# An unused tile of 192 bytes in front of the buffers of k, r and v

## The chip, the cores and the metric

The kernel runs on one core of one Trainium2 chip. The metric is the time of one execution on the device in microseconds (us); shorter is better. The core has five engines with an instruction stream of their own: TensorE (PE; its weight loads are listed as PEld), VectorE (DVE), ScalarE (ACT), GpSimd (POOL) and SyncE (SP), which here only issues DMAs. Tiles lie in the on-chip memory, in 128 partitions; matmul results go to eight PSUM banks, here one tile `banks`.

## The reference

Two layers, in float32, with a batch of B = 4 and S = 768 positions. First an attention with decay over H = 8 heads of D = 48, in which each position multiplies the state by w and adds k times v:

```python
for t in range(S):
    kt, vt, rt = (k[:, :, t], v[:, :, t], r[:, :, t])
    cur = np.einsum('bhd,bhe->bhde', u[None] * kt, vt)
    y[:, :, t] = np.einsum('bhd,bhde->bhe', rt, state + cur)
    state = w[None, :, :, None] * state + np.einsum('bhd,bhe->bhde', kt, vt)
```

Its output, with the heads side by side (384 columns), is the input x of a mixture of four attention experts with a head size of 64: a gate picks two of the four for each position, every expert computes causal softmax attention over the 768 positions, and the results are weighed and summed.

```python
for e in range(E):
    q, k, v = x @ wq[e], x @ wk[e], x @ wv[e]
    scores = np.where(causal, -1e9, scale * (q @ k.transpose(0, 2, 1)))
    a = softmax(scores)
    ye = a @ v @ wo[e]
    out += (weight of e among the two picked, else 0) * ye
```

## The kernel before

The positions are cut into 24 chunks of 128 (6 for each batch element), and these into 8 groups of three. A chunk n goes through the steps of the first layer, whose names begin with `a_`; a group G goes through those of the second, `m_`. A long string, `ORDER`, written out by hand, says in which order the steps issue their instructions, and so fixes the order on each engine. An engine works through its own list and waits on semaphores for what others make. The program gives its DMAs eight semaphores in turn, and an issue waits until the DMA eight before it has landed.

Loads. `load_chunk(n)` loads k (L287) and r (L289) of a chunk, and `load_vh(n)` v (L294), each as 128 partitions (positions) x 8 heads x 48 floats: 1024 rows of 192 bytes. All go through the queue of SyncE. k and r land in `kdbuf` and `rdbuf`, four buffers each, in which a head has 64 floats (256 bytes) of which 48 are filled; v lands in `vhbuf`, four buffers, in which the heads lie side by side (192 bytes each). `load_vs` (L308, L311) fills `vsbuf` with v, its two halves of 64 positions exchanged, for early chunks by a copy on ScalarE and later by DMAs. The weights come through the same queue: wv, wq, wk (`load_v`, `load_qk`) and wo.

The tiles are placed one behind the other in the order in which they are allocated. Ahead of `kdbuf0` this comes to an address of 128 modulo 256 bytes in each partition, and all buffers of k, r and v are multiples of 256 bytes long, so that each starts at 128 modulo 256.

```python
kdbuf = [const.tile([P, H, 64], F32, name=f"kdbuf{i}") for i in range(NK)]
vhbuf = [const.tile([P, H, D], F32, name=f"vhbuf{i}") for i in range(NV4)]
...
nc.sync.dma_start(kt[:, :, :D], k[b, :, s, :].rearrange("h s d -> s h d"))
nc.sync.dma_start(vh, v[b, :, c * C:(c + 1) * C, :].rearrange("h s d -> s h d"))
```

Steps of the first layer that the prediction names: `a_decay` multiplies k and r by tables of powers of w (L483 on GpSimd, L481 on VectorE for the first chunks); `a_ku` (L489, L491 on GpSimd) multiplies k, u and r; `a_transpose` (L519, L512 and L528 for chunk 0) turns k and r on TensorE by means of the identity, and ScalarE copies the result into `kr` (L255, the line of a helper); `a_quarters` (L557, L565), `a_out` (L588, L592) are its matmuls; `a_xt` (L623) turns the result into x. `fill` (L368), `warm_up` (L321) and `keep` (L362) are matmuls without use for the result, which keep TensorE at work at the start. Of the second layer: `hi_qk` (L440) copies wq and wk on ScalarE into a high part `wqk_hi`, the rest becomes `wqk_lo`; `m_values` (L692) and `m_proj` (L664) are projections with three matmuls each, high and low parts of x (`xt_hi`, `xt_lo`) and of the weights; `m_scores` (L742), `m_turn` (L777, with the identity), `m_av` (L798) and `m_out` (L821 to L823) are the attention and its output.

Of the kernel before, what the change touches and what calls it, by code (L numbers as in the profile page):

```python
# [7 lines left out]
F32 = mybir.dt.float32  # L8
# [182 lines left out]
def decay_attention_then_mixture_of_attention(  # L191
# [16 lines left out]
    B, H, S, D = r.shape  # L208
    E, DM, HD = wq.shape
    P = 128  # L210
# [15 lines left out]
    const = ctx.enter_context(tc.tile_pool(name="const", bufs=1))  # L226
# [30 lines left out]
    def load_w():  # L257
# [3 lines left out]
        for side_, rows in enumerate((lo_d, hi_d)):  # L261
            nc.scalar.dma_start(pw[rows, 0, :, 63], w.rearrange("(p two) d -> d two p", two=2)[:, side_])

    kdbuf = [const.tile([P, H, 64], F32, name=f"kdbuf{i}") for i in range(NK)]
    rdbuf = [const.tile([P, H, 64], F32, name=f"rdbuf{i}") for i in range(NR)]

# [615 lines left out]
```

## Time and profile before

| | |
|---|---|
| three runs | 303.3, 304.38, 302.42 us; median 303.3 us |
| the profiled execution | 303.65 us |
| its span, first to last instruction | 301.9 us |
| mean granted clock of TensorE | 0.994 |
| busy: PE, PEld, DVE, ACT, POOL | 96%, 83%, 77%, 61%, 58% of the span |
| read and written in DRAM | 19.28 MB and 4.72 MB |

The profile describes one execution by the hardware profiler. Its times count from the start of the span; the 1.75 us between the span and the execution's time lie before the first and behind the last instruction. Matmuls are pipelined and their ends are modelled, so a busy TensorE is not TensorE at its peak. The share of the DMA engines is a sum of the times of packets, which overlap.

### The profile page before, as it was taken

The page shows a single profiled execution, that of the slowest core. Times are in us where ns is not written, and L with a number is a line of the kernel's source. Part 1 is how long each engine was busy: PE and PEld are TensorE (multiplying, and loading weights), DVE is VectorE, ACT ScalarE, POOL GpSimd, SP SyncE. Part 2 cuts the span into 40 slices and gives each one's busy share as a digit, 9 for nine tenths or more (in the row PEclk, how much of TensorE's full clock was granted, in tenths as well). Part 3 has the DMA queues.
Part 4 walks back from the last instruction along what each step waited for, and adds up shares of the span by engine and source line. Part 5 has one row for each costly group of instructions (what it writes and reads, how often), then busy time and mean ns, then how long its engine had stood idle before and what let it go on. Part 6 is the DMA issues. An engine that isn't in the chain of part 4 may idle for free.

```text
span 301.9 us, 13029 instructions
## 1 busy us (share of the span) xinstructions
PE 291.0 (96%) x5565; PEld 251.1 (83%) x5565; DVE 232.5 (77%) x685; ACT 184.9 (61%) x413; POOL 174.3 (58%) x227
## 2 busy tenths in 40 slices
PE   6997999999999999999999999999999999999985
PEld 3776988898987979898987988997987979987865
DVE  5876498898886987868887788778887498889650
ACT  1864767657686564636867376664695864565722
POOL 1874798967574859376491973674745704226510
PEclk9999899999999999999999999999999999999999
DMA  9987954435088037535361248307070000010202
GB/s 131 180 170 155 158 106 84 79 60 81 28 157 161 2 64 137 111 73 126 80 134 25 48 88 161 73 4 158 12 164 2 28 2 4 0 54 2 77 31 78
DMA packets 103309, 24.83 MB, mean 82 GB/s; under 512 B 99794, under 2 KB 103252, under 8 KB 103252
## 3 DMA queue, kind: packets, MB, share of 16 engines
q1 hardware_dynamic: 102688, 23.90, 42.0%
q8 instruction: 43, 0.70, 1.0%
q10 hardware_dynamic: 564, 0.10, 0.2%
q14 instruction: 14, 0.11, 0.1%
HBM read 19.28 MB, written 4.72 MB: 79 GB/s over the span
## 4 chain that ended last, share of the span: by engine, by line
PE 79%; POOL 7%; DVE 5%; issue 4%; DMA 3%; ACT 0%; ACTq 0%; DVEq 0%; POOLq 0%; SPq 0%
PE banks L664 15%; PE banks L798 13%; PE banks L742 10%; PE banks L692 8%; PE banks L777 7%; PE banks L557 4%; PE banks L519 3%; PE banks L588 3%; PE banks L821 3%; PE banks L592 3%; PE banks L823 3%; PE banks L822 3%; PE banks L565 2%; DMA rdbuf<-in_r_dram 2%; PE banks L623 2%
## 5 line engine op out<-in xcount | busy, mean ns | idle before, releaser
L765 POOL TENSOR_SCALAR pr<-pr,f,gate 128x128 f32<-128x128 f32 (+5 forms) x96 | 68.1, 725 | 62.8 <-DVE f L759 40.1
L752 ACT ACTIVATE pr<-pr,nm 128x384 f32<-128x384 f32 (+5 forms) x96 | 63.2, 662 | 10.2 <-DVE nm L747 9.8
L747 DVE CUSTOM_DVE_ANT_0 pr<-banks,after 128x128 f32<-128x128 f32 (+5 forms) x96 | 55.8, 621 | 13.8 <-PE banks L742 11.3
L255 ACT ACTIVATE pt<-banks 128x768 f32<-128x768 f32 (+2 forms) x40 | 36.0, 910 | 23.6 <-PE banks L777 20.1
L798 PE MATMUL banks<-pt,vv 128*64 128x384 f32 (+2 forms) x324 | 41.5, 393 | 0.9 <-DVE yl L807 0.7
L742 PE MATMUL banks<-tk,tq 64*128 64x384 f32 (+3 forms) x384 | 41.7, 338 | 0.0
L798 PEld LDWEIGHTS banks<-pt,vv 128*64 128x64 f32 x324 | 22.7, 136 | 18.4 <-issue 11.8
L664 PE MATMUL banks<-xt_hi,wqk_hi 128*128 128x384 f32 x96 | 33.7, 351 | 0.0
L664 PE MATMUL banks<-xt_lo,wqk_hi 128*128 128x384 f32 x96 | 32.5, 338 | 0.0
L742 PEld LDWEIGHTS banks<-tk,tq 64*128 64x128 f32 x384 | 31.0, 187 | 1.8 <-issue 0.5
L664 PE MATMUL banks<-xt_hi,wqk_lo 128*128 128x384 f32 x96 | 32.4, 338 | 0.0
L489 POOL TENSOR_TENSOR ku<-kdbuf,uw 128x384 f32<-128x384 f32 x24 | 25.9, 1079 | 9.3 <-DVE banks L498 8.9
L483 POOL TENSOR_TENSOR rdbuf<-rdbuf,tab_r 128x384 f32<-128x384 f32 x22 | 22.5, 1023 | 14.1 <-DMA rdbuf<-in_r_dram 13.7
L777 PEld LDWEIGHTS banks<-ident,pr 64*128 64x128 f32 x672 | 25.4, 139 | 5.1 <-issue 1.8
L777 PE MATMUL banks<-ident,pr 64*128 64x64 f32 x672 | 29.0, 226 | 0.6 <-POOL pr L765 0.2
L588 PE MATMUL banks<-vhbuf,sm 64*64 64x48 f32 x384 | 24.6, 220 | 0.7 <-issue 0.6
L491 POOL TENSOR_TENSOR ku<-ku,rdbuf 128x384 f32<-128x384 f32 x24 | 24.3, 1012 | 1.2
L483 POOL TENSOR_TENSOR kdbuf<-kdbuf,tab_k 128x384 f32<-128x384 f32 x21 | 21.4, 1024 | 5.3 <-DMA kdbuf<-in_k_dram 4.0
L588 PE MATMUL banks<-vsbuf,sm 64*64 64x48 f32 x384 | 24.1, 220 | 0.0
L255 ACT ACTIVATE kr<-banks 128x1024 f32<-128x1024 f32 x19 | 19.4, 1022 | 7.0 <-PE banks L519 6.2
L692 PE MATMUL banks<-wv_hi,xt_hi 128*128 128x260 f32 x72 | 21.9, 304 | 0.0
L588 PEld LDWEIGHTS banks<-vhbuf,sm 64*64 64x64 f32 x384 | 20.5, 134 | 1.1 <-issue 0.9
(132 smaller groups left out, 722.4 us busy)
## 6 DMA issues: line engine op xcount, KB each, us to landing
kdbuf<-in_k_dram SPq DMA_DIRECT2D x24, 192.0 KB, 3.8
rdbuf<-in_r_dram SPq DMA_DIRECT2D x24, 192.0 KB, 4.1
vhbuf<-in_v_dram SPq DMA_DIRECT2D x24, 192.0 KB, 4.1
out_dram<-o SPq DMA_DIRECT2D x23, 192.0 KB, 2.3
vsbuf<-in_v_dram SPq DMA_DIRECT2D x36, 96.0 KB, 3.7
pr<-in_moe_wv_dram SPq DMA_DIRECT2D x1, 384.0 KB, 6.0
pr<-in_moe_wq_dram SPq DMA_DIRECT2D x1, 384.0 KB, 5.7
pr<-in_moe_wk_dram SPq DMA_DIRECT2D x1, 384.0 KB, 6.1
```

The lines of the kernel that those rows point to most:

```text
L255: nc.scalar.activation(to, from_, AF.Copy)
L483: nc.gpsimd.tensor_tensor(t[:, :, :D], t[:, :, :D], (tab_k, tab_r)[which], op=OP.mult)
L489: nc.gpsimd.tensor_tensor(ku, kd[:, :, :D], uw, op=OP.mult)
L588: nc.tensor.matmul(o, st["sm", n][rows, par, p // 2, i], values, start=fresh, stop=True)
L664: nc.tensor.matmul(ps, a[:, t, m0:m0 + P], x[:, t, :], start=i == 0, stop=i == n - 1)
L692: nc.tensor.matmul(ps, x[:, t, cols], a[:, t, :], start=m == 0, stop=m == n - 1)
L742: nc.tensor.matmul(ps[par][:, n0:n1], tq[rows, part, q], tk[rows, key, n0:n1], start=i == 0, stop=i == 2)
L747: nc.vector.tensor_tensor_reduce(pr_[:, :N], ps[par], after[:, S - N:], 1.0, 3e38, op0=OP.add, op1=OP.min, accum_out=nm)
L752: nc.scalar.activation(pr_[:, :N], pr_[:, :N], AF.Exp, bias=nm, scale=-1.0, accum_out=sums[:, e, j, 0:1])
L765: nc.gpsimd.tensor_scalar(p[:, :N], p[:, :N], f[:, i], gate[:, i, e:e + 1], op0=OP.mult, op1=OP.mult)
L777: nc.tensor.transpose(both[:, x, half], mg[G]["p", e, j][rows, i * C:(i + 1) * C], ident[rows, rows])
L798: nc.tensor.matmul(psy[par * HD:par * HD + HD, j0 * C:j1 * C], vv[:, i % GC, e, :], mg[G]["t", e, i][:, (j0 - max(0, i - g * GC)) * C:(j1 ...
```

## The change

One line allocates a tile of 48 floats (192 bytes) in each partition, which nothing uses. All tiles that are allocated after it move by 192 bytes: `kdbuf`, `rdbuf`, `vhbuf` and `vsbuf` from 128 to 64 modulo 256, and likewise, each from its own place, the identity, masks and tables, `uw`, the weights (`wqk_hi`, `wqk_lo`, `wv_hi`, `wv_lo`, `wo_hi`, `wo_lo`, `wg`) and `sums`. The tiles of the string of buffers `BUFS` (`pr`, `tq`, `kr`, `xt_hi` and so on) are allocated before it and stay. The instructions of each engine and their order are the same before and after, so no excerpt of them is shown.

```diff
             nc.scalar.dma_start(pw[rows, 0, :, 63], w.rearrange("(p two) d -> d two p", two=2)[:, side_])
 
+    const.tile([P, D], F32, name="space")
     kdbuf = [const.tile([P, H, 64], F32, name=f"kdbuf{i}") for i in range(NK)]
     rdbuf = [const.tile([P, H, 64], F32, name=f"rdbuf{i}") for i in range(NR)]
```

## Rows read from the trace of the kernel before

**Rows 1.** The page: busy time of TensorE, share of the span, instructions

```profile
PE 291.0 (96%) x5565; PEld 251.1 (83%) x5565; DVE 232.5 (77%) x685; ACT 184.9 (61%) x413; POOL 174.3 (58%) x227
```

**Rows 2.** The page: the chain that ended last, by engine and by line

```profile
PE 79%; POOL 7%; DVE 5%; issue 4%; DMA 3%; ACT 0%; ACTq 0%; DVEq 0%; POOLq 0%; SPq 0%
PE banks L664 15%; PE banks L798 13%; PE banks L742 10%; PE banks L692 8%; PE banks L777 7%; PE banks L557 4%; PE banks L519 3%; PE banks L588 3%; PE banks L821 3%; PE banks L592 3%; PE banks L823 3%; PE banks L822 3%; PE banks L565 2%; DMA rdbuf<-in_r_dram 2%; PE banks L623 2%
```

**Rows 3.** Windows: length; busy PE, PEld, DVE, ACT, POOL; granted clock; DMA share; GB/s

```profile
28.75:32.10 3.35, 3.35 (x49) 2.85 (x39) 1.35 (x3) 0.42 (x2) 2.45 (x3) 0.50 0.51 96
...
36.00:300.00 264.00, 260.78 (x4945) 227.17 (x4943) 208.00 (x627) 165.36 (x375) 151.62 (x191) 1.00 0.35 72
```

**Rows 4.** Timeline of TensorE, 24.5 to 33.3 us (start, length, instructions, [idle before <-releaser])

```profile
25.50 0.26 PE L588 MATMUL banks<-vhbuf,sm 64*64 64x48 f32 x2 [0.57 <-issue]
...
25.99 0.61 PE L368 MATMUL banks<-ident 128*128 128x256 bf16 x4
28.07 0.69 PE L557 MATMUL banks<-kr 48*64 48x64 f32 x32 [1.47 <-ACT kr L255]
28.58 0.77 PE L565 MATMUL banks<-vhbuf,kdbuf 64*48 64x48 f32 x32
...
29.88 0.42 PE L692 MATMUL banks<-wv_hi,xt_lo 128*128 128x260 f32 x1
...
33.16 0.28 PE L692 MATMUL banks<-wv_hi,xt_lo 128*128 128x260 f32 x1
```

**Rows 5.** Timeline of ScalarE, 19 to 29 us

```profile
23.54 0.84 ACT L440 ACTIVATE wqk_hi<-pr 128x768 fp32r<-128x768 f32 x1 [2.34 <-DMA pr<-in_moe_wq_dram]
...
26.26 0.84 ACT L440 ACTIVATE wqk_hi<-pr 128x768 fp32r<-128x768 f32 x1 [1.49 <-DMA pr<-in_moe_wk_dram]
27.01 1.01 ACT L255 ACTIVATE kr<-banks 128x1024 f32<-128x1024 f32 x1
```

**Rows 6.** Timeline of GpSimd, 19 to 40 us

```profile
25.17 0.51 POOL L615 TENSOR_TENSOR z<-z,w 128x192 f32<-128x192 f32 x1
29.65 1.02 POOL L483 TENSOR_TENSOR rdbuf<-rdbuf,tab_r 128x384 f32<-128x384 f32 x1 [3.98 <-DMA rdbuf<-in_r_dram]
...
38.31 1.03 POOL L483 TENSOR_TENSOR rdbuf<-rdbuf,tab_r 128x384 f32<-128x384 f32 x1 [2.35 <-DMA rdbuf<-in_r_dram]
```

**Rows 7.** DMA view, 0 to 13 us in 40 slices of 0.325 us

```profile
GB/s 0 0 0 0 0 9 67 182 253 204 240 137 140 161 175 178 220 209 179 161 164 167 162 161 166 162 163 163 166 161 163 165 175 207 218 212 204 219 181 160
```

**Rows 8.** DMA view, 29 to 36 us in 40 slices of 0.175 us

```profile
GB/s 11 26 26 9 0 0 0 0 46 92 117 192 257 261 236 214 206 170 174 202 204 190 184 171 163 159 134 149 190 187 167 164 160 257 154 150 157 151 161 165
```

**Rows 9.** DMA view, 40 to 53 us in 40 slices of 0.325 us

```profile
GB/s 0 0 67 219 240 114 69 92 225 194 96 120 235 226 244 226 176 162 184 158 79 0 0 0 0 0 0 0 0 25 0 50 34 103 235 233 249 204 91 27
```

**Rows 10.** Timeline of SyncE's queue, 29 to 47 us: issues

```profile
29.43 0.37 SPq L287 DMA_DIRECT2D kdbuf<-in_k_dram  x1
...
39.63 0.37 SPq L294 DMA_DIRECT2D vhbuf<-in_v_dram  x1
...
41.47 1.09 SPq L294 DMA_DIRECT2D vhbuf<-in_v_dram  x1
42.68 0.61 SPq L287 DMA_DIRECT2D kdbuf<-in_k_dram  x1
43.82 0.46 SPq L289 DMA_DIRECT2D rdbuf<-in_r_dram  x1
```

**Rows 11.** Timeline of TensorE, 89 to 92 us

```profile
90.93 0.46 PE L519 MATMUL banks<-ident,rdbuf 64*128 64x64 f32 x8 [0.50 <-POOL rdbuf L483]
```

**Rows 12.** The chain that ended last, in order of time (start, us, what)

```profile
1.71 3.96 DMA pr<-in_w_dram
...
84.45 5.33 DMA rdbuf<-in_r_dram
```

**Rows 13.** Weight loads of TensorE by form (xcount | busy us, mean ns | idle before)

```profile
L664 PEld LDWEIGHTS banks<-xt_lo,wqk_hi 128*128 128x128 f32 x96 | 18.1, 188 | 0.0
...
L822 PEld LDWEIGHTS banks<-wo_lo,yh 128*128 128x128 f32 x50 | 9.4, 188 | 0.0
```

## The prediction

> **What bounds the kernel now.** I read the page first. TensorE is busy for 291.0 of 301.9 us [rows 1], and the chain of work that ended last is 79% TensorE [rows 2]. So a change pays only where it closes a hole in TensorE's row or keeps TensorE's clock up. In the windows by stage, from 36 to 300 us TensorE is busy 260.78 of 264 us at a granted clock of 1.00 [rows 3]: 3.2 us are left in seven eighths of the run. The start is different. In the timeline of TensorE it stands idle for 1.47 us before 28.07, released by ScalarE's kr [rows 4]. From 28.75 to 32.10 the granted clock is 0.50, the lower of the two levels (1.2 against 2.4 GHz) [rows 3]; the fall comes right after that idle time. In it the L692 matmuls take 0.42 us each, at full clock 0.28 [rows 4].
>
> Why was kr late? In ScalarE's timeline the weights' split waits 2.34 us for the load of wq and 1.49 us for that of wk; kr stands right behind [rows 5]. GpSimd waits in the same stretch: 3.98 us for a load of r at 29.65, and 2.35 us for another at 38.31 [rows 6]. So the first 38 us wait for loads, and all loads go through one queue. The program gives its DMAs eight semaphores in turn, so an issue also waits until the DMA eight before it has landed: a load that lands sooner lets later ones start sooner.
>
> How fast does that queue run? In the DMA view of 0 to 13 us a slice is 0.325 us. By slice 19 (6.2 us) the slices sum to about 0.77 MB, nearly four loads of 196,608 bytes (k, r, v, k). Then come 13 slices at 161 to 167 GB/s, 0.69 MB, and behind them five at 204 to 219 [rows 7]; in the order of issue r, k and r stand there, and then two loads of v. The slices count what is read, and reads may run ahead of the writes for part of a load: a burst begins at 240 to 261 GB/s [rows 7, 8] and is then held back. So 163 GB/s is the pace at which rows of k and r are written, and some 212 that of v's. The other views agree. At 29 to 36 us five loads of k and r begin at 257 to 261 GB/s and sink to 134 to 204 [rows 8]. At 40 to 53 us loads of v (issued 39.63 to 41.47) and the front of a k are read at 226 to 244; behind k comes r (issued 42.68 and 43.82), at 158 to 184 [rows 9, 10]. k, r and v have the same shape in DRAM and the same 192-byte rows. What differs is where they land: rows of k and r lie 256 bytes apart from an address of 128 modulo 256, so each covers 128 to 320 and crosses a multiple of 256. Rows of v lie 192 bytes apart, start at 128, 64, 0 and 192 in turn, and half of them cross.
>
> **The change part by part.** *The unused tile.* No instruction writes or reads it, and no instruction is added, removed or reordered on any engine. Its cost is nothing.
>
> *Loads of k and r.* All 48 now land on 64 to 256 and none crosses. If a row costs by the blocks of 256 bytes that it touches, k and r cost 2, and v 1.5: 163 x 2 / 1.5 = 217 GB/s for v, where some 212 is the mean of its slices [rows 7]. One block would give 326 GB/s, which is more than the queue reads where nothing holds it back, 226 to 244 [rows 9]. So I take 212 to 240 GB/s for the new loads: 0.93 to 0.82 us in place of 1.21, and 0.28 to 0.39 us saved for each load in a full queue. That v's rate carries over to k and r is a reading, not shown: no row has k or r without a crossing.
>
> The Trainium skill ("DMA: Bandwidth & Descriptors", section "How a descriptor splits into AXI transactions") says that a descriptor is cut at multiples of 256 bytes, in beats of 32, and that a start off the boundary costs the beats before it too. Counted so, 128 to 320 takes 10 beats and 64 to 256 takes 8; at 163 x 10 / 8 = 204 GB/s a load would save 0.25 us, and the sum below would stand. The section speaks of reads; no row here shows whether it holds where a row is written.
>
> *Loads of v.* They start at 64, 0, 192 and 128: half cross, as before. Nothing.
>
> *The wait at 28.07.* Eight loads of k and r stand in the full queue ahead of the weights: 8 x 0.28 to 0.39 = 2.2 to 3.1 us sooner for wq, wk and what follows. For TensorE not to wait, kr must be done by 26.60, when it ends its fill (25.99 + 0.61) [rows 4]. kr takes 1.01 us and the split 0.84 [rows 5], so wk must be there by about 24.7, where it came at 26.2: 1.5 us sooner is enough. The whole 1.47 us go. ScalarE's own work leaves room (free at 21.2 us, 23.54 less the wait, and 2.0 us of work ahead of kr), so 0.7 to 1.6 us are to spare.
>
> *The clock.* With no hole before 28 us I take the fall as gone: 3.4 us at half clock (28.7 to 32.1) hold 1.7 us of full-clock work, so 1.7 us are saved. Bounds: 0 if it falls anyway, 1.7 if not. It is nearer to 1.7, because the one fall between 8 us and the end follows the one long hole.
>
> *Does the rest keep up?* GpSimd's r at 29.65 comes 2.2 to 3.9 us sooner (eight to ten loads); GpSimd is free at 25.7 [rows 6], so it gains at least 2.2. The r at 38.31 is the last of five k and r loads; the first of them is issued at 29.43 [rows 10], when TensorE's L565 of 28.58 [rows 4] has read the k of its buffer. That is 1.5 to 2 us sooner, and five loads give 1.4 to 2.0 more: 2.9 to 4.0. TensorE's 3.2 us can therefore be kept.
>
> *Later.* The hole of 0.50 us at 90.93 waits for GpSimd's rdbuf [rows 11], and that for a load of r that took 5.33 us [rows 12] with another r just ahead: two loads save 0.56 to 0.78, so the hole goes.
>
> *The front.* The chain begins with the small load of w, 3.96 us from issue [rows 12], queued among the first k and r: 0 to 0.5 us. I take 0, because ScalarE and a cold TensorE have work of their own there. The 0.57 us at 25.50 have no releaser [rows 4]: 0 to 0.57, taken as 0.
>
> *Operands.* Identity, masks, tables and weights move by 192 bytes too. A weight load from wqk (224 modulo 256) takes 188 ns and one from yh (128) 188 ns [rows 13]: nothing.
>
> Sum: 1.47 + 1.7 + 0.50 = 3.7 us off the profiled execution's 303.65 us: 299.95. Its own time stands 0.35 us above the median of the runs, 303.3, well inside their spread (302.42 to 304.38). I forecast **300.0 us**, 1.1% less. At best, with both terms taken as 0, it is 303.65 - 4.75 = 298.9.
>
> **The rivals.** *It speeds the loads less, or the clock falls anyway.* If a load saves 0.1 us, the hole shrinks by 0.8 and stays: 302.9. If the hole goes but the clock falls: 303.65 - 1.97 = 301.7. For it: the rows show the fall behind the hole, not that it comes from it alone. Range 301.3 to 302.9.
>
> *The change doesn't do what it says: the gap between rows, or their size, is what costs.* Rows of k and r leave 64 bytes free after each 192; v's rows do not. This explains 163 against 212 just as well. Then nothing moves and the time is 303.3. The Trainium skill (same page, "Specifications") has a rule on this side: transfers under 512 bytes are done as read-modify-write. 192 bytes stay under that at any address, and by that rule alone the time stays at 303.3; that v, with rows of the same size, runs at 212 speaks for the address having a part.
>
> *Slower: the operands that moved.* Transposes (L777, L519, L623) read the identity, now at 64 in place of 128. L777 and L519 alone hold 10% of the chain [rows 2], 31 us. If crossings are free and those take 10% longer, that is +3.1 us: 306.8. It outweighs the forecast's gain only beyond 12%. Rows 13 speak against it.
>
> **How the numbers follow.** A measurement of this kernel can tell about 1% (3 us) from no change. Forecast (298.9 to 301.3): 0.51. Smaller gain (301.3 to 302.9): 0.16. No change (302.4 to 304.4): 0.28. Slower (about 306.8): 0.05. The bound of 1% is 300.3, just above the forecast; of its 0.51 I put 0.37 below. The rest of it, the smaller gain and no change make 0.58 within 1%. The range runs from 298.8 (the forecast's best) to 303.9 (most of no change): it leaves out the slower case, the upper edge of no change and a little below, under 0.2.
>
> **What would show it.** In the DMA view of 0 to 13 us the slices at 161 to 167 become 204 or more; the loads of k show a shorter time to landing. ScalarE's waits for wq and wk shrink by 2 us or more together; the hole at 28.07 is gone, the granted clock stays at 1.00 past 28 us, and GpSimd's 3.98 us shrink below 2. Wrong would be: slices still at 163 (no change); faster loads with a hole as before (the queue was not what wk waited for); or a hole that opens at another place between 30 and 50 us, with the clock falling there.

## The result, and the profile after

| | before | after |
|---|---|---|
| median of 7 runs each, taken side by side | 303.92 us (302.42 to 304.69) | 300.32 us (298.62 to 301.77) |
| ratio after / before | | 0.9883, 95% interval 0.9844 to 0.9921 |
| the profiled execution, its span | 303.65, 301.9 us | 301.08, 299.3 us |
| busy TensorE, granted clock | 291.0 us, 0.994 | 287.7 us, 1.00 |

The change saves 1.2%, 3.6 us by the medians; the forecast was 300.0 us. The two profiled executions are 2.6 us apart, since the one of before is 0.3 us below its median and that of after 0.8 above, so what follows accounts for 2.6 us. The profile shows which of the terms behind the forecast held. Lines of code behind the new one stand one further down: L664 of before is L665 here.

The DMA view of 0 to 13 us, 40 slices of 0.325 us, answers to [rows 7]:

```profile
GB/s 0 0 0 0 0 11 92 185 247 178 238 213 179 233 242 193 201 199 206 234 197 171 174 193 219 240 151 142 203 202 189 214 193 244 206 182 193 190 203 211
```

The 13 slices at 161 to 167 are gone. Slices 20 to 32 (6.2 to 10.4 us) have a mean of 195 GB/s, where it was 163. The step on the pace held in direction, and fell short of the 212 to 240 that were taken.

ScalarE's timeline, 20 to 27 us, answers to [rows 5]:

```profile
22.14 0.85 ACT L441 ACTIVATE wqk_hi<-pr 128x768 fp32r<-128x768 f32 x1 [1.75 <-DMA pr<-in_moe_wq_dram]
...
24.77 0.84 ACT L441 ACTIVATE wqk_hi<-pr 128x768 fp32r<-128x768 f32 x1 [1.40 <-DMA pr<-in_moe_wk_dram]
25.52 1.00 ACT L255 ACTIVATE kr<-banks 128x1024 f32<-128x1024 f32 x1
```

wq comes 1.40 us sooner, wk 1.49 us; but what ScalarE has ahead of them came sooner too, so that the two waits shrank by 0.68 us together, not by 2. TensorE's timeline, 24 to 32 us, answers to [rows 4]:

```profile
24.13 0.26 PE L589 MATMUL banks<-vhbuf,sm 64*64 64x48 f32 x2 [0.34 <-issue]
...
26.57 0.69 PE L558 MATMUL banks<-kr 48*64 48x64 f32 x32 [1.34 <-ACT kr L255]
...
28.02 0.28 PE L693 MATMUL banks<-wv_hi,xt_hi 128*128 128x260 f32 x1
...
30.05 0.47 PE L520 MATMUL banks<-ident,kdbuf 64*128 64x64 f32 x8 [0.81 <-POOL kdbuf L484]
```

The hole before kr is still there: 1.34 us, where 1.47 stood before. And yet the clock doesn't fall behind it: L693 takes 0.28 us. A hole of 0.81 us that before did not have follows at 30.05. The windows say the same of the clock (length; busy PE, PEld, DVE, ACT, POOL; granted clock; DMA share; GB/s), beside [rows 3]:

```profile
28.75:32.10 3.35, 2.54 (x35) 2.25 (x34) 2.30 (x3) 2.09 (x4) 3.28 (x5) 1.00 1.02 204
36.00:295.00 259.00, 256.43 (x4923) 222.99 (x4922) 207.40 (x624) 162.51 (x367) 149.65 (x188) 1.00 0.33 71
```

GpSimd's timeline, 22 to 40 us, answers to [rows 6]: its two waits for r are 3.25 and 0.81 us, where they were 3.98 and 2.35.

```profile
28.01 1.02 POOL L484 TENSOR_TENSOR rdbuf<-rdbuf,tab_r 128x384 f32<-128x384 f32 x1 [3.25 <-DMA rdbuf<-in_r_dram]
...
34.61 1.02 POOL L484 TENSOR_TENSOR rdbuf<-rdbuf,tab_r 128x384 f32<-128x384 f32 x1 [0.81 <-DMA rdbuf<-in_r_dram]
```

The chain in order of time begins with the small load of w, as in [rows 12], now 3.14 us from issue in place of 3.96:

```profile
1.72 3.14 DMA pr<-in_w_dram
```

That load is issued by ScalarE while the first k and r are under way, and the chain goes on by VectorE and GpSimd to TensorE's L417 (L416 in the kernel before, at 9.90 us):

```profile
7.02 0.94 POOL L387 TENSOR_TENSOR w<-pr 128x2 f32<-128x2 f32 x3 [4.84 <-DVE pr L381]
...
9.08 0.91 PE L417 MATMUL banks<-pt,ones 1*128 1x384 f32 x2 [0.48 <-POOL lower L348]
```

Where is the time gained? TensorE's matmuls stand in the same order in both kernels (some small ones of L588 and L592, interleaved, apart), so the start of one and the same matmul can be compared. The table has the starts of five, in us from the start of the span:

| matmul | before | after | sooner |
|---|---|---|---|
| the 61st, first layer's values (11.25) | 11.25 | 10.43 | 0.82 |
| the 541st, behind the hole before kr | 28.64 | 27.14 | 1.50 |
| the 601st, in the first `m_values` | 33.16 | 31.05 | 2.11 |
| the 1201st | 57.68 | 54.66 | 3.02 |
| the last | 298.63 | 296.03 | 2.60 |

All of it is gained by 57 us: 0.8 us at the front; 0.7 up to kr, of which 0.13 is the hole before kr, 0.23 the idle time at 25.50 [rows 4] (0.57 us, now 0.34) and 0.29 comes between two matmuls of L588 at 20.67; 0.6 by the 601st; 0.9 between 33 and 57 us, 0.7 of that in three steps of 0.2 to 0.3 us at 48 to 52 us.

What sets the 0.6? In the kernel before, the transposes behind the stretch at half clock start at 32.17 us, with no idle time listed ahead of them. In this one they wait 0.81 us for GpSimd's kdbuf, and start 2.04 us after GpSimd takes up the r that it had waited for (28.01). A kernel of the experiments below, k and r at 192, has the pace of before and a clock of 1.00 throughout; there too it is 2.04 us (TensorE of before; GpSimd and TensorE of k and r at 192, where L519 is L521):

```profile
32.17 0.47 PE L519 MATMUL banks<-ident,kdbuf 64*128 64x64 f32 x8
```

```profile
29.86 1.01 POOL L485 TENSOR_TENSOR rdbuf<-rdbuf,tab_r 128x384 f32<-128x384 f32 x1 [4.11 <-DMA rdbuf<-in_r_dram]
```

```profile
31.90 0.46 PE L521 MATMUL banks<-ident,kdbuf 64*128 64x64 f32 x8 [1.22 <-POOL kdbuf L485]
```

So in the kernel before, where GpSimd takes up that r at 29.65 [rows 6], these transposes could have started at 31.69 at the earliest, whatever the clock: the fall held them up by 0.5 us. Of the 2.1 us gained here, 1.6 are those by which the r comes sooner.

Later the hole at 90.93 [rows 11] is gone, but two new ones, at 58.85 (no releaser) and at 119.97 (for VectorE's copy into an output buffer), take more than that away:

```profile
58.85 0.28 PE L693 MATMUL banks<-wv_lo,xt_hi 128*128 128x260 f32 x1 [0.58 <-issue]
...
119.97 1.05 PE L743 MATMUL banks<-tk,tq 64*128 64x384 f32 x6 [0.69 <-DVE o L253]
```

### The profile page after: what moved, and what is told of

The parts are those of the page before. It is cut to its first block, busy times and chain, and to the rows that moved or that the text cites. A ratio compares the mean times of both kernels' runs of the same rounds, so it can differ in the third digit from the quotient of the medians.

```text
span 299.3 us, 13029 instructions
## 1 busy us (share of the span) xinstructions
PE 287.7 (96%) x5565; PEld 248.3 (83%) x5565; DVE 233.3 (78%) x685; ACT 184.7 (62%) x413; POOL 173.1 (58%) x227
## 4 chain that ended last, share of the span: by engine, by line
PE 85%; POOL 5%; issue 3%; DMA 2%; DVE 2%; ACT 2%; ACTq 0%; POOLq 0%; DVEq 0%
PE banks L665 17%; PE banks L799 13%; PE banks L743 11%; PE banks L693 9%; PE banks L778 7%; PE banks L558 4%; PE banks L520 4%; PE banks L589 3%; PE banks L593 3%; PE banks L822 3%; PE banks L824 3%; PE banks L823 3%; PE banks L566 2%; PE banks L624 2%; POOL ku L490 2%
## 5 line engine op out<-in xcount | busy, mean ns | idle before, releaser
L665 PE MATMUL banks<-xt_hi,wqk_hi 128*128 128x384 f32 x96 | 33.5, 349 | 0.0
L665 PE MATMUL banks<-xt_hi,wqk_lo 128*128 128x384 f32 x96 | 32.3, 337 | 0.0
L665 PE MATMUL banks<-xt_lo,wqk_hi 128*128 128x384 f32 x96 | 32.3, 337 | 0.0
L490 POOL TENSOR_TENSOR ku<-kdbuf,uw 128x384 f32<-128x384 f32 x24 | 25.0, 1040 | 10.3 <-DVE banks L499 10.0
L589 PE MATMUL banks<-vhbuf,sm 64*64 64x48 f32 x384 | 24.4, 219 | 0.3 <-issue 0.3
L693 PE MATMUL banks<-wv_hi,xt_hi 128*128 128x260 f32 x72 | 21.5, 299 | 0.0
```

Source lines behind the costliest of these rows:

```text
L490: nc.gpsimd.tensor_tensor(ku, kd[:, :, :D], uw, op=OP.mult)
L589: nc.tensor.matmul(o, st["sm", n][rows, par, p // 2, i], values, start=fresh, stop=True)
L665: nc.tensor.matmul(ps, a[:, t, m0:m0 + P], x[:, t, :], start=i == 0, stop=i == n - 1)
L693: nc.tensor.matmul(ps, x[:, t, cols], a[:, t, :], start=m == 0, stop=m == n - 1)
```

## The experiments

### Which of the moved tiles, and which address

Four kernels came first. The first moves k and r alone and puts all else back:

```diff
+    const.tile([P, 48], F32, name="space")
     kdbuf = [const.tile([P, H, 64], F32, name=f"kdbuf{i}") for i in range(NK)]
     rdbuf = [const.tile([P, H, 64], F32, name=f"rdbuf{i}") for i in range(NR)]
+    const.tile([P, 16], F32, name="space_after")
```

> Only the buffers of k and r lie at 64 modulo 256; a second unused tile of 64 bytes behind them puts v, identity, masks, tables and weights back where they were. If crossings of k and r are the cause: as with the whole change, ratio 0.988 (0.984 to 0.992), slices of the DMA view of 0 to 13 us at 190 to 240 GB/s instead of 163, granted clock 1.0 or nearly. If the other tiles that moved have the gain: ratio 1.000, slices at 163 with k and r no matter.

The second leaves k and r at 128 and moves the rest (the 48 floats stand behind `rdbuf`):

> k and r stay at 128 modulo 256, all tiles behind them move by 192 bytes as in the change. If crossings of k and r are the cause: ratio 1.000 (0.996 to 1.004), slices at 161 to 167 GB/s, clock 0.994. If the other tiles have the gain: ratio 0.988.

The third and the fourth are the first with other numbers, so that k and r start at 0, or at 96, modulo 256, and all else stays where it was:

> k and r at 0 modulo 256, all else as before: rows cover 0 to 192, no crossing. By blocks of 256 bytes: as with the change, ratio 0.988, slices at 190 to 240. By beats of 32 bytes counted from the block's start (6 here, 8 at 64, 10 at 128): the same or a little better, since reads set the pace. If 64 were good for another reason than the crossing: 1.000 and 163.

> k and r at 96 modulo 256, all else as before: rows cover 96 to 288 and cross by 32 bytes. By blocks touched: as before the change, 161 to 167 GB/s and ratio 1.000. By beats counted from the block's start (9, against 10 at 128): 163 x 10 / 9 = 181 GB/s and about half the gain, 0.994.

| k and r at | the rest | median, us | ratio to before | mean of slices 20 to 32, GB/s |
|---|---|---|---|---|
| 64 | as before | 300.47 | 0.9889 (0.9802 to 0.9976) | 209 |
| 128 | moved | 303.8 | 0.9993 (0.9955 to 1.0031) | 163 |
| 0 | as before | 301.05 | 0.9876 (0.9811 to 0.9941) | 208 |
| 96 | as before | 304.52 | 1.0007 (0.9972 to 1.0043) | 163 |

The DMA view of 0 to 13 us of k and r at 64 and the rest as before, then of k and r at 128 and the rest moved:

```profile
GB/s 0 0 0 0 0 10 74 188 251 195 230 217 188 224 226 164 163 159 232 232 236 227 226 174 177 242 195 234 223 148 179 223 207 187 193 210 175 171 184 211
```

```profile
GB/s 0 0 0 0 0 12 88 174 248 201 213 167 151 183 166 186 218 201 173 161 165 165 162 164 165 162 163 163 165 162 163 165 186 209 217 217 192 202 167 226
```

Of k and r at 0:

```profile
GB/s 0 0 0 0 0 14 75 194 238 204 218 208 184 251 233 193 207 174 177 243 226 157 171 192 213 248 223 184 194 199 225 226 197 166 218 196 238 215 173 203
```

and at 96:

```profile
GB/s 0 0 0 0 0 12 88 193 240 208 232 149 140 165 164 188 216 207 177 160 162 167 161 164 164 161 164 164 164 164 162 166 178 212 219 216 217 215 183 180
```

The gain comes from k and r alone, and it comes at both addresses at which a row of 192 bytes stays inside one block of 256 bytes (64 to 256, 0 to 192). The moved identity, masks and weights neither cost nor give anything that can be told from no change (0.9955 to 1.0031). At 96 a row crosses by only 32 bytes and the pace is the same 163 GB/s as at 128, where it crosses by 64: what counts is that a second block is touched.

An experiment of the last set belongs here, k and r at 192, where the row is cut into 64 and 128 bytes (16 floats ahead of `kdbuf`, 48 behind `rdbuf`):

> The kernel before, with k's and r's buffers at 192 modulo 256, v and all else at 128: a row covers 192 to 384 and is cut into 64 and 128 bytes, where it was 128 and 64, and 160 and 32 with the buffers at 96. Theory A (a row costs by the blocks of 256 bytes that it touches, two in all three cases): slices at 161 to 167 GB/s from about 6.5 us on, no change of the time, ratio 0.996 to 1.004. Rival B (a row costs by 32-byte steps counted from the last multiple of 256 ahead of it, 12 here, 10 in the kernel before): 136 GB/s, and 2 us slower or more, 306 or above. Rival C (how the row is cut matters, the first piece above all): a pace other than 161 to 167 GB/s.

304.49 us, ratio 1.0003 (0.9973 to 1.0032), and a mean of 164 GB/s:

```profile
GB/s 0 0 0 0 0 14 65 190 250 215 225 141 144 169 166 188 214 202 175 153 170 171 165 164 164 162 164 163 164 163 164 164 181 208 218 212 191 209 173 179
```

So theory A: two blocks cost the same however the row is cut between them. The Trainium skill ("DMA: Bandwidth & Descriptors", section "How a descriptor splits into AXI transactions") has both counts: a descriptor is cut into transactions at multiples of 256 bytes, and each transaction costs beats of 32 bytes from the multiple below its start. By the beats the rows at 128, 96 and 192 would take 10, 9 and 12, and from 163 GB/s at 128 follow 181 and 136 (estimates by that page). The runs show 163 and 164: the cut into transactions agrees, the beats do not count here. The section speaks of reads; these rows are cut where they are written.

### k alone, r alone

```diff
+    const.tile([P, 48], F32, name="space")
     kdbuf = [const.tile([P, H, 64], F32, name=f"kdbuf{i}") for i in range(NK)]
+    const.tile([P, 16], F32, name="space_after")
     rdbuf = [const.tile([P, H, 64], F32, name=f"rdbuf{i}") for i in range(NR)]
```

> The kernel before, with k's buffers alone moved to 64 modulo 256 (the unused 192 bytes ahead of them, 64 more unused bytes ahead of r's buffers); r, v and all else stay at 128. So half the loads of the change are freed of crossings. Theory A (the gain is a sum over loads that each get faster): half of it, 301.9 to 302.6 us, with slices of the DMA view between the two paces, and the front 0.3 to 0.5 us sooner. Rival B (only r counts, as the waits of GpSimd for r and the hole at 90.93 suggest): the time stays at 303.3 to 304.2. Rival C (k alone takes the first chunks out of the way): the whole gain, 300.0 to 301.

301.39 us, ratio 0.9905 (0.9873 to 0.9938): three quarters of the gain, between theory A and rival C; the interval reaches into both ranges. Then the other half, with the 48 floats ahead of `rdbuf` and the 16 behind it:

> The kernel before, with r's buffers alone moved to 64 modulo 256; k, v and all else stay at 128 modulo 256. It is the other half of the kernel with k alone, which gave 2.75 of the 3.6 us. Theory A (each load that is freed adds its own part): the rest, 0.9 us, so 302.8 to 303.5. Rival B (the queue needs only to be fast enough, and either half does most of it): 301.0 to 302.0, and the two halves add up to more than the whole. Rival C (k alone matters): 303.7 to 304.3.

300.74 us, ratio 0.9878 (0.9834 to 0.9922): all of it, though the intervals of the two halves overlap, so that which half gives more is not shown. They give 2.75 and 3.9 us (against the runs of before beside each), 6.7 in sum, and together they give 3.6: the gain is not a sum over loads. Theory A of the second experiment falls, and the time is a little below the range of its rival B, with that rival's sum. The DMA views of 0 to 13 us, with k alone and with r alone at 64, bear on why:

```profile
GB/s 0 0 0 0 0 9 97 201 249 188 242 211 205 200 203 218 235 213 173 239 215 212 229 190 203 187 165 191 216 246 248 224 219 199 165 181 245 274 172 229
```

```profile
GB/s 0 0 0 0 0 5 89 199 243 201 239 189 191 235 241 251 238 173 172 177 216 236 236 196 185 232 225 232 191 201 246 228 197 214 178 167 170 183 262 266
```

Slices 20 to 32 have a mean of 215 GB/s, with k alone 213, with both 195 to 213 (six profiles). From 163 GB/s for two blocks, one block would give 326, and k and r in turn, one of each kind, 2 / (1/163 + 1/326) = 217 GB/s. That is an estimate, and it meets the 213 and 215. With both at one block the pace should then rise to some 275 GB/s and not to 326: by the sums of the slices, 1.5 of the 4.2 loads that are read in these slices are v's, of which half the rows still cross. It doesn't rise at all. Something else, which no run here isolates, holds the queue at some 195 to 215 GB/s, and the second half of the change adds nothing that these runs show.

### Does order do the same? The loads of wq and wk sooner

The hole of 1.34 us stayed because wq and wk stand behind two loads of v and one of k. The next kernel is the changed one with this move (parts of the long lines are left out):

```diff
-fill,7/7 a_xt,1/0 load_v/2 hi_v load_vh,3 a_decay,3,0 a_ku,3/1
+fill,7/7 a_xt,1/0 load_v/2 hi_v load_qk,1/0 load_qk,0/4 load_vh,3 a_decay,3,0 a_ku,3/1
...
-load_vh,4 load_qk,1/0 hi_qk,1 load_vs,4 load_qk,0/4 hi_qk,0
+load_vh,4 hi_qk,1 load_vs,4 hi_qk,0
```

> The changed kernel, with the two loads of wq and wk moved in SyncE's order: issued right behind the gate's weights (wg), ahead of two loads of v and one of k; nothing else moves on any engine. In the changed kernel wq is issued at 16.41 and wk at 18.72 us, ScalarE waits 1.75 and 1.40 us for them, and TensorE then 1.34 us for kr at 26.57. Theory A (the hole is left because wq and wk stand behind three other loads and the ring of eight semaphores, not because their bytes are slow): both issue 1.5 to 2 us sooner, both waits of ScalarE vanish, the hole at 26.57 is gone, and 300.3 becomes 298.5 to 299.5. Rival B (the queue is the limit whatever its order): the loads of v and k that now come behind 0.79 MB of weights are late by as much, the hole moves to whoever needs them, and the time stays at 300.0 to 301. Rival C: the loads of r that follow come later too, GpSimd's wait of 3.25 us grows, and the time rises above 301.

301.1 us, ratio to before 0.9878 (0.9819 to 0.9936): no better than the change alone. ScalarE's timeline, 22 to 28 us:

```profile
24.22 0.36 ACT L309 ACTIVATE vsbuf<-vhbuf 64x192 f32<-64x192 f32 x1 [3.15 <-DMA vhbuf<-in_v_dram]
24.61 0.84 ACT L441 ACTIVATE wqk_hi<-pr 128x768 fp32r<-128x768 f32 x1
25.36 1.00 ACT L255 ACTIVATE kr<-banks 128x1024 f32<-128x1024 f32 x1
```

Neither wq nor wk is waited for any more, and the same time goes into one wait of 3.15 us for the v that now comes behind them; kr starts 0.16 us sooner than in the changed kernel, and TensorE's hole before it is 1.36 us. This is rival B's picture, with a time 0.1 us above its range. GpSimd's first wait for r shrinks from 3.25 to 1.52 us, and its second grows from 0.81 to 4.07, a part of rival C. The same move in the kernel before:

> The kernel before, with the same move of the loads of wq and wk ahead of two loads of v and one of k; k, r and v stay at 128 modulo 256. Theory A (what the change gave in the middle of the start comes from wk landing sooner, so that order can take the place of faster loads): the hole of 1.47 us at 28.07 goes, the front (first matmul of L416 at 9.90 us) stays, and 303.9 becomes 302.0 to 302.8, not the 300.3 of the change. Rival B (the bytes count, not their order): k and r for the next chunks come later by as much, and the time stays at 303.5 to 304.5.

306.0 us, ratio 1.0048 (1.0008 to 1.0088), slower, and outside both theories. ScalarE's timeline and GpSimd's, 22 to 31 us:

```profile
26.32 0.36 ACT L308 ACTIVATE vsbuf<-vhbuf 64x192 f32<-64x192 f32 x1 [4.35 <-DMA vhbuf<-in_v_dram]
```

```profile
30.65 1.02 POOL L483 TENSOR_TENSOR rdbuf<-rdbuf,tab_r 128x384 f32<-128x384 f32 x1 [5.07 <-DMA rdbuf<-in_r_dram]
```

The waits for v and r grew to 4.35 and 5.07 us, the hole before kr to 2.01. In this stretch everything that the queue brings is wanted at once, so order only says who waits; as far as these runs go, more bytes by a given time is what helps. By 13 us, 1.97 MB have been read in the kernel before and 2.20 MB in the changed one (the sums of the slices).

### What is the fall of the clock worth?

The kernel before, with eight more useless matmuls in the hole (the start of the line is left out):

```diff
-a_add,2 fill,9/4
+a_add,2 fill,9/4 fill,11/4 fill,12/4
```

> The kernel before, with two more fills on TensorE (each four matmuls without use, 0.61 us) right behind the fill that starts at 25.99 us, so that the hole of 1.47 us in front of 28.07 is filled for 1.2 us; no load and no other engine is touched. Of 18 runs of the kernel before beside the first four kernels, ten had a mean clock of 1.0 (median 303.8 us) and eight one of 0.992 to 0.994 (median 304.7). Theory A (the fall of the clock behind 28 us follows from the hole, as predicted): no run falls, all have a clock of 1.0 and the time is 303.0 to 303.8. Rival B (the fall comes with or without it, since a kernel with a hole of 1.60 us kept its clock): some runs still show 0.992 to 0.994 and the time stays at 303.9. Either way the time stays well above 300.3: the clock gives at most 1 us of the 3.6.

305.7 us, ratio 1.0041 (1.0011 to 1.0072): slower, and outside both theories' ranges. Nine of its ten runs have a mean clock of 0.998 or more. Of 60 runs of the kernel before, taken beside the experiments, 26 have that, with a median of 304.1 us, and 34 less (0.994 at most), with a median of 304.5. So the hole has a part in the fall (fewer falls when it is filled), but it doesn't decide it: k and r at 96 kept the clock behind a hole of 1.60 us, and 26 runs of before kept it. And by these medians the fall costs some 0.4 us of the whole, not 1.7; even the 0.4 is not clear of the runs' spread. TensorE's timelines of the kernel with fills, at 25 to 32 us and at 53 to 63 us:

```profile
25.93 1.49 PE L368 MATMUL banks<-ident 128*128 128x256 bf16 x12
28.21 0.69 PE L557 MATMUL banks<-kr 48*64 48x64 f32 x32 [0.79 <-ACT kr L255]
...
31.66 0.46 PE L519 MATMUL banks<-ident,kdbuf 64*128 64x64 f32 x8 [0.79 <-POOL kdbuf L483]
...
53.66 0.28 PE L777 MATMUL banks<-ident,pr 64*128 64x64 f32 x3 [1.11 <-issue]
```

The transposes that stand at 32.17 us in the kernel before start at 31.66 here, 0.51 us sooner, after 0.79 us of waiting for GpSimd: with the clock kept up, this is all that GpSimd leaves. The 601st matmul of before, here the 609th, starts at 32.65, still 0.51 us ahead, and the 1201st, here the 1209th, at 58.45, 0.77 us behind. New idle times without a releaser lie between, the longest of 1.11 us, and one of 1.20 us follows at 62.45; why they come was not tried.

### One execution or the kernel?

The kernels with k, or r, or both at 64 and the rest left had no hole before kr in their profiles (r alone: wk's wait 0.37 us, kr at 24.18). So the changed kernel was profiled again:

> The changed kernel once more, unaltered, to see which of its lines belong to the kernel and which to one execution. Its first profile (301.08 us) has ScalarE waiting 1.75 and 1.40 us for wq and wk and a hole of 1.34 us at 26.57, while the kernels with k and r alone, or k alone, moved waited 0.46 and 0.41 us or so and had no such hole (299.8 to 301.4 us). Theory A (the hole belongs to the kernel): waits of 1.2 to 1.8 us and a hole of 1.0 to 1.5 us again. Rival B (how early wq and wk land differs from execution to execution): waits below 0.8 us in sum each and a hole below 0.6 us, with a time of the profiled execution below 300.5 us. In both the slices at 161 to 167 GB/s are absent, the first matmul of L417 stands before 9.6 us, and the median is 299.5 to 301.

300.26 us, ratio 0.9865 (0.9809 to 0.9921). The profiled execution took 302.72 us and TensorE's timeline has the hole again:

```profile
26.22 0.69 PE L558 MATMUL banks<-kr 48*64 48x64 f32 x32 [1.47 <-ACT kr L255]
```

That is theory A's hole, though of ScalarE's waits, 1.77 and 1.04 us, the second is below its range. But both profiled executions of the changed kernel (301.08 and 302.72) are among the longer of its 11 runs, 298.42 to 302.72 with a median of 300.32. The kernels without the hole were profiled at 299.76, 300.02 and 300.1 us, and k and r at 0, with a hole of 1.07 us, at 302.43. One thing differs between them: in the three without the hole SyncE's long issue is that of wk (2.19 to 2.90 us), and ScalarE has wk by 22.8 to 23.4 us; in the two of the changed kernel it is that of wq (2.27 and 1.88), and wk comes at 24.8 and 24.4. Whether placement or the execution decides is open.

### What holds the queue at 11 to 16 us

SyncE's timeline of the changed kernel and its DMA view of 13 to 26 us, 40 slices of 0.325 us:

```profile
10.96 0.70 SPq L451 DMA_DIRECT2D pr<-in_moe_wv_dram  x1
11.71 2.53 SPq L452 DMA_DIRECT2D wg<-in_moe_w_gate_dram  x1
14.29 0.49 SPq L295 DMA_DIRECT2D vhbuf<-in_v_dram  x1
...
16.41 2.27 SPq L438 DMA_DIRECT2D pr<-in_moe_wq_dram  x1
18.72 1.09 SPq L438 DMA_DIRECT2D pr<-in_moe_wk_dram  x1
...
21.25 2.58 SPq L465 DMA_DIRECT2D pr<-in_moe_wo_dram  x1
```

```profile
GB/s 253 273 282 224 61 32 35 54 79 195 293 225 236 191 164 158 163 74 19 61 118 213 282 291 277 247 178 224 255 244 249 229 162 52 20 153 111 334 268 297
```

Behind the issue of wg the queue sinks to 32 GB/s, and again to 19 and 20 behind the issues of 2.27 and 2.58 us (wq, wo). In 8 of these 40 slices it moves 61 GB/s or less, and there a faster load can gain little. The kernel before has the same: its issue of wg takes 2.90 us, and the queue sinks to 29 GB/s behind it. The last kernel takes wg from the queue (parts of the long lines, and the new step's entry in the list of steps, are left out):

```diff
-        nc.sync.dma_start(wg, w_gate.rearrange("(t p) e -> p t e", t=KT))
+    def load_g():
+        nc.scalar.dma_start(wg, w_gate.rearrange("(t p) e -> p t e", t=KT))
...
-load_vh,2 a_xt,0/3 a_own,1/71 load_chunk,3
+load_vh,2 a_xt,0/3 load_g a_own,1/71 load_chunk,3
```

> The changed kernel, with the load of the gate's weights (wg, 6 KB in pieces of 16 bytes) taken from SyncE's queue and issued by ScalarE, in its idle time of 1.40 us before 17.39 us; no other instruction moves. In both profiles of the changed kernel SyncE's issue of wg took 2.53 and some 3.0 us (11.71 to 14.24, 11.61 to 14.6), and behind it the queue sank to 16 to 61 GB/s from about 14.3 to 15.6 us, before v, k, v, wq and wk followed. Theory A (that issue is what now holds the weights back, not the pace of any load): v follows wv at once, wq and wk are issued 1.5 to 2.5 us sooner, ScalarE's waits for them (1.75 and 1.40, 1.77 and 1.04 us) fall below 0.5 each, the hole of 1.34 to 1.47 us before kr is gone, and 300.3 becomes 299.0 to 299.8, about what the fastest executions of the changed kernel show (298.4 to 299.1). Rival B (an issue takes as long as the queue is full, whichever load it is): the time moves to the issue of the next load, wq and wk come as before, 300.0 to 300.8. Rival C (wg lands too late for ScalarE's copy at 19.42, or its issue holds ScalarE up): 301 or more.

299.52 us (299.28 to 299.95 in four runs), ratio to before 0.9851 (0.9811 to 0.9891). The time is in theory A's range, SyncE's timeline is rival B's:

```profile
10.74 1.31 SPq L451 DMA_DIRECT2D pr<-in_moe_wv_dram  x1
12.09 2.44 SPq L295 DMA_DIRECT2D vhbuf<-in_v_dram  x1
14.66 0.64 SPq L288 DMA_DIRECT2D kdbuf<-in_k_dram  x1
```

The long issue is now that of v, so it isn't wg's own: the load that stands behind wv waits there. wq is issued 0.19 us sooner, wk 0.53, and the hole before kr is 1.07 us. It is the fastest kernel here by its median, but its interval overlaps the changed kernel's, so that it is faster is not shown.

## Why the prediction was right, step by step

**The cause held.** The pace of 163 GB/s was read as that of rows that touch two blocks of 256 bytes. The addresses 0, 64, 96, 128 and 192 bear it out: 163 or 164 where a row crosses, 195 to 213 where none of k and r does. The rival that the gaps between rows or their size cost falls, since these are the same at all five. The Trainium skill's rule on transfers under 512 bytes ("DMA: Bandwidth & Descriptors", "Specifications"), which stood behind that rival, cannot tell them apart: 192 bytes are under it at each address. The rival of the moved operands falls too: with them alone moved the ratio is 0.9993.

**Loads, 0.28 to 0.39 us each: too high.** 163 to 195 in the profile of after is 0.2 us for each of 196,608 bytes, 163 to 215 would be 0.29. One block was rightly not taken at 326 GB/s, but the limit that takes over lies at 195 to 215, not at 212 to 240. So the condition of the rival "It speeds the loads less" was met in part, and the hole stayed as it says; its time, 301.3 to 302.9 us, did not come, since time was won at places that neither the forecast nor it had counted. (By the prediction's own division its estimate of 204 GB/s saves 0.24 us, not 0.25, and its best case is 298.9, not the 298.8 of its range; nothing hangs on either.)

**The hole before kr, -1.47: failed.** 0.13 us in the profile. The prediction let all of the eight loads' gain, 2.2 to 3.1 us, reach wk; 1.5 us reached it. And the need for wk moved too: 0.82 us had come at the front, and TensorE ended its fill at 25.23 us, where it was 26.60, 1.37 us sooner. 1.50 less 1.37 is the 0.13. And past 11.7 us the issues, more than the pace, set when wk comes: the long ones of wg and wq (2.53 and 2.27 us) leave the queue nearly empty twice before wk. (That is read from the timelines; no run here takes the long issues away.) A target that is fixed ("wk by 24.7") was the mistake: what waits had itself been waiting for faster loads. "Faster loads with a hole as before" stands in the prediction's own list of what would show it wrong. In both profiles of the changed kernel this came true; the forecast's time came out all the same, by other ways.

**The clock, -1.7: failed, in its reason and in its size.** The hole stayed and the fall went all the same, and more than two fifths of the runs of before had no fall. The step took all the time lost at half clock as saved, as if TensorE alone set the pace from 28.7 to 32.1 us. GpSimd's kdbuf, behind the wait for r, comes next: without the fall the kernel before could have started its transposes at 31.69 in place of 32.17, 0.5 us sooner, and the kernel with fills, whose clock stayed up, gained 0.51 there. At a clock of 0.998 or more, before has a median of 304.1 and after 300.2 us: the gain is all there without the clock.

**The front, 0: failed the other way.** 0.82 us, above the bound of 0.5. The load of w (3.14 us, not 3.96) runs beside the first k and r, and all that stands behind it came sooner by as much. The step looked at ScalarE and TensorE, which have work of their own there; but the way leads by VectorE and GpSimd, which wait for it, to TensorE's L416, which is idle before it.

**GpSimd's r, below 2 us: failed**, 3.25 us, for the reason of wk's: it came 1.64 us sooner, not 2.2 to 3.9. The second r came 3.70 us sooner (34.61 for 38.31), within the 2.9 to 4.0. The prediction asked only whether GpSimd keeps up; in the traces its first r decides what TensorE gains by 33 us.

**"3.2 us are left from 36 us on, and can be kept": too narrow.** From 33 to 57 us 0.9 us more are gained. From the 1201st matmul to 3.6 us before the last one, by the windows of both, TensorE is idle for 2.57 us now (54.66 to 292.40 us, busy 235.17) and was idle for 1.82 (57.68 to 295.00, busy 235.50): part of what is won at the start is given back in the new holes at 58.85 and 119.97.

**The hole at 90.93, -0.50: held.**

So the sum of 3.7 us met a gain of 3.6, with 3.2 of it in two steps that did not work as told, and the front, GpSimd's r and the stretch up to 57 us in their place. The cause, the sign and the stage (the start, by its waits for loads) were right; that the sum agrees to 0.1 us is luck.

## What to carry to other kernels

The rows of 192 bytes loaded here should not cross a multiple of 256 bytes in the on-chip memory; for other short rows it is worth trying. Look at the address of a buffer modulo 256 and at the pitch of its rows, and read the pace of loads from the slices of a queue that is full. When loads get faster, move every consumer's need forward too before counting what is left of a wait, and ask how much speed is enough: here either half of the loads gave most of the gain, and the queue became no faster with both. Before counting a faster clock as time saved, look at which engine the next step waits for. Reordering a queue whose every load is wanted at once only names another victim.

## What the runs showed of the hardware

- A load of 192-byte rows is written at 163 to 164 GB/s if each row touches two blocks of 256 bytes, cut 160 + 32, 128 + 64 or 64 + 128 alike.
- With the rows of k and r inside one block, or those of either alone, the queue read 195 to 215 GB/s, not twice 163; the cause of this limit is open.
- SyncE's issue of the load behind wv took 2.53 us for the 6 KB of wg and, with wg taken away, 2.44 for v; behind it the queue sank to 32 to 61 GB/s for 1.3 us, and to 35 for 0.65. It was as short as 1.16 us with k alone at 64; what sets it is open.
- The granted clock fell to 0.50 for 3.4 us behind an idle time of 1.47 us in the profile of before, and stayed at 1.00 behind one of 1.34 in that of after. In the kernel before 34 of 60 runs have a mean of 0.994 or less, and 26 of 0.998 or more.
